# A two-axis FFT mixing followed by a squared-ReLU feed-forward: the row d = 128 is spread over the partitions by way of DRAM, two more windows form P−Q+N on VectorE, and two small copies go to GpSimd

## The chip, the cores and the metric

The kernel runs on one core of one Trainium2 chip. The metric is the device time of one execution in microseconds; the time before is 608.82 us, the median of three runs (608.44 to 608.91). A core has TensorE (PE in the profile; PEld is its weight load), VectorE (DVE), ScalarE (ACT), GpSimd (POOL) and SyncE (SP). Each engine takes its instructions in the order in which they were issued to it; semaphores join the engines. DMAs are issued from the queues of SP, ACT and POOL.

## The reference, cut to what matters

```python
# x: (8, 3008, 256) f32; w_in: (256, 2048); w_out: (2048, 256)
X = fft(fft(x, axis=1), axis=2)           # over the 3008 positions, then over the 256 channels
y = X.real.reshape(8 * 3008, 256)         # 24,064 tokens
h = maximum(y @ w_in, 0)
out = h * h @ w_out                       # (24064, 256) f32
```

The kernel computes it in f16 with f32 accumulation. A real input makes the two FFTs symmetric: frequency k and frequency S − k need the same two products, and the output column for k uses their one combination and that for S − k the other. So the kernel works on 12,040 columns (one for each pair k, S − k of every batch element) and writes two output rows from nearly every column.

## The kernel before, in words

**Order.** There is no scheduler: the order in which the Python code issues instructions is the order on each engine. The kernel cuts the 12,040 columns into 25 *windows* (`wins`, w = 0 to 24): 240, 512, 376, 376, 512 and 448 columns first, then 512 each, the last 360. Counted from one, windows 3 and 4 are the fourth and the fifth block. A window is worked through in eight *steps* s = 0 to 7; one step makes two of the sixteen 128-row groups of the hidden layer.

**What a step does.** For its two groups a plain step runs `pq(s)` (L825: four matmuls, cosine part P from `zc` and sine part Q from `zs`, 512 columns each in a full window, into the PSUM tile `ph`), then `relu(s, 0)` on ScalarE (L861) for the columns k, later `turn(s)` (L849: two more matmuls that subtract the sine part twice and add the row d = 128 with the other sign) and `relu(s, 1)` for the columns S − k; `power` (L866) squares on VectorE. Between these stand sixteen matmuls of the second layer of the window before (`ffn2_steps`, L687; twelve where that window has 376 columns), its evictions `osb` (L702) and stores (L667, on SP's queue), and a share of the work that prepares later windows (`others`, L879).

**P−Q+N steps.** In the steps listed in `diff` (L728, L760 to L763) the two `turn` matmuls are not run. There `cosines(s)` (L834) makes P alone, `twice(s)` on VectorE (L840) computes t2 = N − 2P while only P is in PSUM, `sines(s)` (L844) adds Q, and `relu(s, 1)` becomes one VectorE instruction (L859) that adds t2 and the PSUM tile and cuts at zero. `sines` has to wait for `twice`, because it overwrites what `twice` reads. The square of the first half then goes to ScalarE (`power_act`, L870), that of the second half stays on VectorE. Before, `diff` lists (4, 6) for windows 4 and 5, (0, 2, 4, 6) for most later ones, (2, 4, 6) for windows 8, 10, 13, 16 and 19, and (0, 2) for window 9: 73 such steps.

**N.** N is the contribution of the row d = 128, which sits in partition 0 of `zs` (twice, with the weight row of that channel): for hidden row f and column n it is g2n[f] · zs[0, n]. `spread_nyq(wt)` (L777) spreads partition 0 of window wt's `zs` over all 128 partitions: a matmul with the selector `sel` (L781, into a PSUM tile `pn` of the pool of two that the z matmuls use) and a copy on ScalarE (L782) into `zn`. `nyq_rows(wt, steps)` (L784) makes from it, on GpSimd, the two products of a step (L790) in a tile `n2`; there are three such buffers, so the rows of one step wait until `twice` of the third step before has read its own. `nyq` (L892) says when: for a window whose step 0 is in `diff`, `hi` is 5, the spread and the rows of its first step are issued at step 5 of the window before, the others at steps 6 and 7. For a window that starts its list at 2 it is one step later, and windows 4 and 5 do it at their own step 0.

**z.** The columns of a later window (`zc`, `zs`) are made by the z matmuls (L572) of `z_steps`, spread over the steps from `lo` up to but not including `hi` (L798; windows 3 and 4 set their own `lo` and `hi`, L813 and L817), with evictions on ScalarE (L577, L583) and VectorE (L601).

**Folds.** The even frequencies of a batch element i go through DRAM once: `away` (L456) writes `ev`, `back` (L464, L466) reads it in two orders, both on GpSimd's queue, as do the loads of x (L127, L132). `fold8`, `fold16` and `nyq8` (L473 to L497) follow on VectorE; `nyq8`, two copies of four elements per partition, is issued at step 0 of the window two after the one with `away`, and the z matmuls of that unit read what it writes.

Of the kernel before, what the change touches and what calls it, by code (L numbers as in the profile page):

```python
# [9 lines left out]
F32 = mybir.dt.float32  # L10
F16 = mybir.dt.float16
I32 = mybir.dt.int32
AF = mybir.ActivationFunctionType
# [3 lines left out]
P = 128  # L17
# [3 lines left out]
def rev_dim(ap, i):  # L21

    dims = [list(d) for d in ap.ap]
    step, cnt = dims[i]
    dims[i] = [-step, cnt]
    return bass.AP(tensor=ap.tensor, offset=ap.offset + step * (cnt - 1), ap=dims)
# [3 lines left out]
def kernel(  # L30
# [14 lines left out]
    nc = tc.nc  # L45
    B, S, D = x.shape
# [9 lines left out]
    WN = 512  # L56
# [23 lines left out]
    NW = len(wins)  # L80

    def win_of(col):
        return max(w for w in range(NW) if wins[w][0] <= col) if col < TOT else NW
# [5 lines left out]
    col_of = {}  # L89
# [11 lines left out]
    const = ctx.enter_context(tc.tile_pool(name="const", bufs=1))  # L101
# [9 lines left out]
    drp = ctx.enter_context(tc.tile_pool(name="drp", bufs=2, space=bass.MemoryType.DRAM))  # L111
    ps_h = ctx.enter_context(tc.tile_pool(name="ps_h", bufs=2, space=bass.MemoryType.PSUM))
    ps_o = ctx.enter_context(tc.tile_pool(name="ps_o", bufs=2, space=bass.MemoryType.PSUM))
    ps_z = ctx.enter_context(tc.tile_pool(name="ps_z", bufs=2, space=bass.MemoryType.PSUM))
# [72 lines left out]
    spn = fop.tile([P, 2, 2, P], F16, name="spn")  # L187
# [128 lines left out]
    for i in (1, 0):  # L316
        nc.gpsimd.tensor_scalar(out=perm[i], in0=prow_i, scalar1=float(P - 1 - i), scalar2=None, op0=ALU.is_equal)
    nc.gpsimd.dma_start(out=wout16, in_=moe_w_out.rearrange("(c p) o -> p c o", p=P))
    sel = const.tile([P, P], F16, name="sel")
    nc.gpsimd.memset(sel, 0.0)  # L320
    nc.gpsimd.memset(sel[0:1, :], 1.0)
    pick = const.tile([P, 1], F16, name="pick")
    nc.gpsimd.memset(pick, 0.0)
    nc.gpsimd.memset(pick[0:1, :], -2.0)
# [42 lines left out]
    def fold_steps(i):  # L367
# [15 lines left out]
        lo = xf[:, :, 1:129]  # L383
        hi = rev_dim(xf[:, :, 128:256], 2)
# [108 lines left out]
        def nyq8():  # L493

            xt, yt = st["xt"], st["yt"]
            nc.vector.tensor_copy(xt[:, 0, :, :, 130:131], rev_dim(rev_dim(xt[:, 1, :, :, 128:129], 1), 2))
            nc.vector.tensor_copy(spn[:, :, :, 0:1], rev_dim(yt[:, :, 0, :, 128:129], 1))  # L497

        late = [lambda: fold8(0), lambda: fold8(1), lambda: fold16(0), lambda: fold16(1), nyq8]
        return {"u_odd": u_odd, "u_part": u_part, "v_even": v_even, "v_part": v_part, "d_even": d_even, "n_cos": n_cos, "odds": odds, "d_odd": d_odd, "load": load, "n_sin": n_sin, "nyq": nyq, "even": even, "away": away, "back": back, "late": late}  # L500

    gh = const.tile([P, 3, F], F16, name="gh")
# [35 lines left out]
    def zwin(w):  # L538
        if w not in zc:
            zc[w] = zp.tile([P, WN], F16, name="zc", tag="zc")  # L540
            zs[w] = zp.tile([P, WN], F16, name="zs", tag="zs")
        return zc[w], zs[w]
# [182 lines left out]
    NST = NFC // 2  # L725
    at_of = {w: [[] for _ in range(NST)] for w in range(NW)}
    post_of = {w: [[] for _ in range(NST)] for w in range(NW)}
    diff = {w: (0, 2, 4, 6) if w > 5 else (4, 6) for w in range(4, NW)}  # L728

    def put(w, s, i, name, *k, d=at_of):  # L730
        d[w][s].append(lambda: folds[i][name](*k))
# [32 lines left out]
    n2s = {}  # L764
# [12 lines left out]
    def spread_nyq(wt):  # L777
        wn1 = wins[wt][1]
        zn = zns[wt] = znp.tile([P, WN], F16, name="zn", tag="zn")
        pn = ps_z.tile([P, 512], F32, name="pn", tag="pz")  # L780
        nc.tensor.matmul(pn[:, 0:wn1], sel, zwin(wt)[1][:, 0:wn1], start=True, stop=True)  # L781
        nc.scalar.activation(zn[:, 0:wn1], pn[:, 0:wn1], AF.Copy, bias=0.0, scale=1.0)  # L782

    def nyq_rows(wt, steps):  # L784
        wn1 = wins[wt][1]
        for s in steps:
            n2 = n2s[wt, s] = wp.tile([P, 2, WN], F32, name="n2", tag="w16")
            for a in range(2):
                fc = 2 * s + a
                nc.gpsimd.tensor_scalar(out=n2[:, a, 0:wn1], in0=zns[wt][:, 0:wn1], scalar1=g2n[:, fc : fc + 1], scalar2=1.0, op0=ALU.mult, op1=ALU.mult)  # L790

    old = None
    for w in range(NW):
# [1 line left out]
        h2 = h2p.tile([P, NFC, 2 * WN], F16, name="h2", tag="h2")  # L795
        zcw, zsw = zwin(w)

        lo, hi = int(any(win_of(col_of[i, 1]) == w + 1 for i in range(2, B))), NST - 3 if 0 in diff.get(w + 1, ()) else NST - 2  # L798
        at, post = at_of[w], post_of[w]
        if w == 1:  # L800
            fj = fold_jobs(1)
# [6 lines left out]
        elif w == 3:  # L808
# [4 lines left out]
            lo, hi = 3, NST - 1  # L813
        elif w == win_of(col_of[1, 1]) - 1:
            for st in range(5):
                at[min(st, 3)] += folds[1]["late"][st : st + 1]
            lo, hi = 4, NST - 1  # L817
# [72 lines left out]
                    j()  # L890

        def nyq(s):  # L892
            if w + 1 in diff and hi < NST - 1:
                if s == hi:
                    spread_nyq(w + 1)
                    nyq_rows(w + 1, diff[w + 1][0:1])
                elif s == hi + 1:
                    nyq_rows(w + 1, diff[w + 1][1 : 2 if s < NST - 1 else None])
                elif s == hi + 2:
                    nyq_rows(w + 1, diff[w + 1][2:])  # L900
            if s == 0 and w in diff and w not in zns:
                spread_nyq(w)
                nyq_rows(w, diff[w])

        def quad(p):
            ph = phs[p] = ps_h.tile([P, 2, 512], F32, name="ph", tag="psh")
            for c in range(4):
                f0 = (4 * p + c) * P
                o = ph[:, c // 2, (c % 2) * wn : (c % 2 + 1) * wn]
                nc.tensor.matmul(o, gh[:, 0, f0 : f0 + P], zcw[:, 0:wn], start=(c % 2 == 0), stop=False, skip_group_check=True)  # L910
                nc.tensor.matmul(o, gh[:, 1, f0 : f0 + P], zsw[:, 0:wn], start=False, stop=True, skip_group_check=True)
# [54 lines left out]
        for s in range(NST) if w > 1 else ():  # L966
            held["on"] = s + 1 in diff.get(w, ()) or (s + 1 == NST and 0 in diff.get(w + 1, ()))
            if s in diff.get(w, ()):
                cosines(s)
                twice(s)  # L970
                settle()
                others(s)
                sines(s)
                first(s)
                relu(s, 1)
                keep(s, 1, 2)
                plus.append(lambda s=s, p=power_act: p(s))
                nyq(s)
                continue
            pq(s)  # L980
            settle()
            first(s)
            if s == NST - 1:
                power(s, 0, 1)
            others(s)
            nyq(s)
            turn(s)
            relu(s, 1)
            keep(s, int(s == NST - 1), 2)
# [36 lines left out]
```

## Time and profile before

The profiled execution took 607.33 us, of which the profile spans 605.5 us; the median of the three runs shown is 608.82 us.

| | |
|---|---|
| time, median of three | 608.82 us |
| profiled execution / its span | 607.33 / 605.5 us |
| granted TensorE clock | 0.999 of full speed |
| spreading matmuls (L781) | 21 |
| copies of the spread row (L782) | 21, 616 ns each at 512 columns |
| products n2 (L790) | 146 |
| `twice` (L842) / relu on VectorE (L859) | 73 / 73 |
| copies of `nyq8` (L496, L497) | 8 and 8, 3.5 and 1.8 us in all |

The page of the profile gives the busy time of each engine, a strip of 40 time slices, the DMA queues, the chain of work that ended last, and groups of instructions by source line; the trace answers by line, tile and stretch of time. Matmuls are pipelined, so that the time one takes from its neighbour is the distance of their starts, not the length shown.

### The profile page before, as it was taken

To read this page: it belongs to the slowest core of one execution; us is meant where nothing else is said; L and a number is where in the kernel's file an instruction comes from. 1 tells how busy PE (TensorE), PEld (TensorE's weight loads), DVE (VectorE), ACT (ScalarE), POOL (GpSimd) and SP (SyncE) were. 2 spreads that over 40 slices of the span, in tenths; PEclk is the share of its full clock that TensorE was granted. 3 is DMA by queue.
4 is the path that set the end of the run, shared out by engine and by line. 5 is a ranking of instruction groups with operands and counts; after the bars stand their busy time and mean duration, and the time that the engine had idled before them with its cause. 6 is when DMAs were issued, how large, how long until landed. Compare 5 with 4: busy or idle time off the path is not lost.

```text
span 605.5 us, 11294 instructions
## 1 busy us (share of the span) xinstructions
PE 591.2 (98%) x4449; PEld 427.9 (71%) x4449; DVE 490.1 (81%) x593; ACT 462.8 (76%) x634; POOL 213.6 (35%) x249
## 2 busy tenths in 40 slices
PE   7899999999999999999999999999999999999997
PEld 3457786776777777777777767777677777777786
DVE  8787656987998878979889799888988988777760
ACT  6697777968888787877787878787777787878762
POOL 8320223245504506365045451363431522513300
PEclk9999999999999999999999999999999999999999
DMA  8945321127111361271113711146112311111112
GB/s 150 155 90 136 115 71 34 39 94 150 52 49 40 114 140 52 77 166 48 52 37 109 146 53 36 40 125 134 44 30 86 88 35 39 51 46 38 54 57 69
DMA packets 36524, 47.52 MB, mean 78 GB/s; under 512 B 4215, under 2 KB 30327, under 8 KB 36471
## 3 DMA queue, kind: packets, MB, share of 16 engines
q0 software_dynamic: 9344, 22.14, 17.9%
q1 hardware_dynamic: 26899, 24.44, 13.5%
q8 instruction: 35, 0.57, 0.4%
q10 hardware_dynamic: 228, 0.21, 0.1%
q14 instruction: 18, 0.15, 0.1%
HBM read 33.63 MB, written 27.84 MB: 102 GB/s over the span
## 4 chain that ended last, share of the span: by engine, by line
PE 87%; DVE 9%; ACT 2%; issue 1%; POOL 0%; DVEq 0%; POOLq 0%; ACTq 0%
PE po L687 49%; PE ph L852 8%; PE ph L829 7%; PE ph L830 7%; PE ph L847 5%; PE ph L838 5%; PE pz L572 4%; DVE h L868 3%; DVE t L842 2%; DVE h L859 2%; DVE xy L491 1%; PE pn L781 1%; ACT h L923 1%; ACT h L861 0%; DVE m L243 0%
## 5 line engine op out<-in xcount | busy, mean ns | idle before, releaser
L687 PE MATMUL po<-wout,h 128*128 128x256 f16 (+1 forms) x3024 | 362.3, 273 | 0.0
L861 ACT ACTIVATE h<-ph 128x1024 f16<-128x1024 f32 (+3 forms) x311 | 295.5, 993 | 79.0 <-PE ph L847 59.1
L687 PEld LDWEIGHTS <-h 128*128 128x128 f16 (+1 forms) x3024 | 296.8, 98 | 72.0
L790 POOL TENSOR_SCALAR n<-zn,g2n 128x512 f32<-128x512 f16 (+2 forms) x146 | 144.2, 1002 | 256.3 <-ACT zn L782 248.4
L868 DVE TENSOR_TENSOR h<-h 128x1024 f16<-128x1024 f16 (+6 forms) x216 | 203.2, 951 | 30.0 <-ACT h L861 27.5
L859 DVE CUSTOM_DVE_ANT_0 h<-t,ph 128x1024 f16<-128x1024 f32 x67 | 81.7, 1220 | 31.6 <-ACT h L861 31.5
L842 DVE SCALAR_TENSOR_TENSOR t<-ph,n 128x1024 f32<-128x1024 f32 (+2 forms) x73 | 87.7, 1202 | 23.4 <-PE ph L838 22.1
L829 PE MATMUL ph<-zc,gh 128*128 128x512 f16 (+3 forms) x238 | 87.4, 368 | 0.4 <-ACT h L923 0.3
L830 PE MATMUL ph<-zs,gh 128*128 128x512 f16 (+3 forms) x238 | 87.4, 368 | 0.0
L872 ACT ACTIVATE h<-h 128x1024 f16<-128x1024 f16 (+2 forms) x73 | 76.5, 1048 | 0.0
L852 PE MATMUL ph<-zs,gh 128*128 128x512 f16 (+3 forms) x238 | 68.1, 368 | 0.2 <-ACT h L861 0.2
L702 ACT ACTIVATE osb<-po 128x512 f32<-128x512 f32 (+3 forms) x95 | 55.5, 589 | 10.6 <-PE po L687 9.7
L847 PE MATMUL ph<-zs,gh 128*128 128x512 f16 (+2 forms) x146 | 42.7, 374 | 1.4 <-DVE t L842 1.2
L838 PE MATMUL ph<-zc,gh 128*128 128x512 f16 (+2 forms) x146 | 42.8, 375 | 0.4 <-DVE h L859 0.4
L830 PEld LDWEIGHTS <-gh 128*128 128x128 f16 x238 | 23.2, 98 | 25.7 <-issue 0.9
L829 PEld LDWEIGHTS <-gh 128*128 128x128 f16 x238 | 23.2, 97 | 25.0
L577 ACT ACTIVATE es<-pz 128x376 f32<-128x376 f32 (+1 forms) x32 | 14.9, 486 | 16.4 <-PE pz L572 16.3
L852 PEld LDWEIGHTS <-gh 128*128 128x128 f16 x238 | 22.3, 98 | 6.2 <-issue 0.3
L838 PEld LDWEIGHTS <-gh 128*128 128x128 f16 x146 | 14.3, 98 | 17.2 <-issue 0.6
L456 POOL DMA_DIRECT2D scr<-ev x8 | 4.9, 616 | 58.3 <-DVE ev L452 52.5
L466 POOL DMA_INDIRECT rb<-scr,idx_r x16 | 18.2, 1140 | 4.9 <-issue 4.9
L132 POOL DMA_INDIRECT xo<-in_x_dram,idx_r x15 | 16.3, 1090 | 4.5 <-issue 4.3
(145 smaller groups left out, 368.5 us busy)
## 6 DMA issues: line engine op xcount, KB each, us to landing
out_dram<-osb SPq DMA_DIRECT2D x77, 128.0 KB
xo<-in_x_dram POOLq DMA_DIRECT2D x7, 768.0 KB
scr<-ev POOLq DMA_DIRECT2D x8, 390.0 KB, 2.9
rb<-scr POOLq DMA_DIRECT2D x16, 130.0 KB
out_dram<-osb SPq DMA_DIRECT2D x12, 94.0 KB
w<-in_moe_w_in_dram POOLq DMA_DIRECT2D x2, 512.0 KB
wout<-in_moe_w_out_dram POOLq DMA_DIRECT2D x1, 1024.0 KB, 11.9
out_dram<-osb SPq DMA_DIRECT2D x8, 75.0 KB
```

What stands on the lines that cost most here:

```text
L687: nc.tensor.matmul(po[0:m, j * D : (j + 1) * D], h2[:, fc, q : q + m], wout16[:, fc, :], start=(fc == 0), stop=(fc == NFC - 1))
L790: nc.gpsimd.tensor_scalar(out=n2[:, a, 0:wn1], in0=zns[wt][:, 0:wn1], scalar1=g2n[:, fc : fc + 1], scalar2=1.0, op0=ALU.mult, op1=ALU.mult)
L829: nc.tensor.matmul(ph[:, a, 0:wn], gh[:, 0, f0 : f0 + P], zcw[:, 0:wn], start=True, stop=False)
L830: nc.tensor.matmul(ph[:, a, 0:wn], gh[:, 1, f0 : f0 + P], zsw[:, 0:wn], start=False, stop=True)
L838: nc.tensor.matmul(ph[:, a, 0:wn], gh[:, 0, f0 : f0 + P], zcw[:, 0:wn], start=True, stop=True)
L842: nc.vector.scalar_tensor_tensor(out=t2[:, :, 0:wn], in0=phs[s][:, :, 0:wn], scalar=-2.0, in1=n2s[w, s][:, :, 0:wn], op0=ALU.mult, op1=ALU ...
L847: nc.tensor.matmul(phs[s][:, a, 0:wn], gh[:, 1, f0 : f0 + P], zsw[:, 0:wn], start=False, stop=True, skip_group_check=True)
L852: nc.tensor.matmul(phs[s][:, a, 0:wn], gh[:, 2, f0 : f0 + P], zsw[:, 0:wn], start=False, stop=True, skip_group_check=True)
L859: nc.vector._custom_dve(TENSOR_ADD_SAT, out=h, in0=t2s[s][:, :, 0:wn], in1=phs[s][:, :, 0:wn], s0=BIG, s1=0.0)
L861: nc.scalar.activation(h, phs[s][:, :, 0:wn], AF.Relu, bias=0.0, scale=-1.0)
L868: nc.vector.tensor_tensor(h, h, h, op=ALU.mult)
L872: nc.scalar.activation(h, h, AF.Square, bias=0.0, scale=1.0)
```

## The change

Four things are edited. (1) `spread_nyq` no longer uses TensorE: ScalarE's queue writes the row, `zs[0:1, 0:wn1]`, to a small DRAM tile `rd` (two buffers), and GpSimd's queue reads it back with a partition step of 0, so that all 128 partitions of `zn` get it. The selector `sel` is gone. (2) The steps move: `hi` is 4 for windows before one with step 0 in `diff` (it was 5) and 5 for the others in `diff` (it was 6); the rows of the first step are issued one step after the spread, those of the second one step later again, the rest at step 7 or, where the steps run out, at step 0 of the window itself. (3) `diff` gets the steps (2, 4, 6) for window 3, which had none, and for window 4, which had (4, 6). (4) `nyq8` runs on GpSimd for batch elements i > 1.

```diff
-    sel = const.tile([P, P], F16, name="sel")
-    nc.gpsimd.memset(sel, 0.0)
-    nc.gpsimd.memset(sel[0:1, :], 1.0)
...
-            nc.vector.tensor_copy(xt[:, 0, :, :, 130:131], rev_dim(rev_dim(xt[:, 1, :, :, 128:129], 1), 2))
-            nc.vector.tensor_copy(spn[:, :, :, 0:1], rev_dim(yt[:, :, 0, :, 128:129], 1))
+            eng = nc.gpsimd if i > 1 else nc.vector
+            eng.tensor_copy(xt[:, 0, :, :, 130:131], rev_dim(rev_dim(xt[:, 1, :, :, 128:129], 1), 2))
+            eng.tensor_copy(spn[:, :, :, 0:1], rev_dim(yt[:, :, 0, :, 128:129], 1))
...
-    diff = {w: (0, 2, 4, 6) if w > 5 else (4, 6) for w in range(4, NW)}
+    diff = {w: (0, 2, 4, 6) if w > 5 else (4, 6) if w == 5 else (2, 4, 6) for w in range(3, NW)}
...
-        pn = ps_z.tile([P, 512], F32, name="pn", tag="pz")
-        nc.tensor.matmul(pn[:, 0:wn1], sel, zwin(wt)[1][:, 0:wn1], start=True, stop=True)
-        nc.scalar.activation(zn[:, 0:wn1], pn[:, 0:wn1], AF.Copy, bias=0.0, scale=1.0)
+        rd = drp.tile([1, WN], F16, name="rd", tag="rd")
+        nc.scalar.dma_start(out=rd[:, 0:wn1], in_=zwin(wt)[1][0:1, 0:wn1])
+        nc.gpsimd.dma_start(out=zn[:, 0:wn1], in_=bass.AP(tensor=rd.tensor, offset=rd.offset, ap=[[0, P], [1, wn1]]))
...
-        lo, hi = ..., NST - 3 if 0 in diff.get(w + 1, ()) else NST - 2
+        lo, hi = ..., NST - 4 if 0 in diff.get(w + 1, ()) else NST - 3 if w + 1 in diff else NST - 2
...
         def nyq(s):
-            if w + 1 in diff and hi < NST - 1:
+            if w + 1 in diff:
                 if s == hi:
                     spread_nyq(w + 1)
-                    nyq_rows(w + 1, diff[w + 1][0:1])
                 elif s == hi + 1:
-                    nyq_rows(w + 1, diff[w + 1][1 : 2 if s < NST - 1 else None])
+                    nyq_rows(w + 1, diff[w + 1][0:1])
                 elif s == hi + 2:
+                    nyq_rows(w + 1, diff[w + 1][1:2])
+                elif s == hi + 3:
                     nyq_rows(w + 1, diff[w + 1][2:])
             if s == 0 and w in diff and w not in zns:
                 spread_nyq(w)
                 nyq_rows(w, diff[w])
+            elif s == 0 and w in diff:
+                nyq_rows(w, [q for q in diff[w] if (w, q) not in n2s])
```

In the instruction lists of the two programs, TensorE loses 29 matmuls: the 21 spreads, two `turn` matmuls of 512 columns (window 4, step 2) and six of 376 (window 3). ScalarE loses 21 copies and gains 22 DMA issues, VectorE loses twelve small copies and gains four `twice` and four L859 instructions, and GpSimd gains 22 DMA issues, twelve small copies and eight products.

More of the change, by code (lines that the diff above doesn't have):

```diff
@@ L796 @@
         zcw, zsw = zwin(w)
-        lo, hi = int(any(win_of(col_of[i, 1]) == w + 1 for i in range(2, B))), NST - 3 if 0 in diff.get(w + 1, ()) else NST - 2
+        lo, hi = int(any(win_of(col_of[i, 1]) == w + 1 for i in range(2, B))), NST - 4 if 0 in diff.get(w + 1, ()) else NST - 3 if w + 1 in diff else NST - 2
         at, post = at_of[w], post_of[w]
@@ L892, in nyq @@
         def nyq(s):
-            if w + 1 in diff and hi < NST - 1:
+            if w + 1 in diff:
                 if s == hi:
                     spread_nyq(w + 1)
+                elif s == hi + 1:
                     nyq_rows(w + 1, diff[w + 1][0:1])
-                elif s == hi + 1:
-                    nyq_rows(w + 1, diff[w + 1][1 : 2 if s < NST - 1 else None])
                 elif s == hi + 2:
+                    nyq_rows(w + 1, diff[w + 1][1:2])
+                elif s == hi + 3:
                     nyq_rows(w + 1, diff[w + 1][2:])
```

## The prediction

> **What bounds the kernel.** I read the page's busy times first, then the chain that ended last, then the waits, then the stretches of time around the places that the change touches.
>
> ```profile
> PE 591.2 (98%) x4449; PEld 427.9 (71%) x4449; DVE 490.1 (81%) x593; ACT 462.8 (76%) x634; POOL 213.6 (35%) x249
> ...
> PE 87%; DVE 9%; ACT 2%; issue 1%; POOL 0%; DVEq 0%; POOLq 0%; ACTq 0%
> ```
>
> TensorE is busy 98% and carries 87% of the chain. A busy figure of pipelined matmuls may hide idle time, so I took the starts of all matmuls from the trace: 109 ns apart at 256 columns and 216 ns at 512, in unbroken series. What exceeds that between neighbours is 16.4 us in all, but only 3.4 us of it after 100 us. From there to the end the kernel is a stream of matmuls without holes, and a matmul taken out is worth its slot, if nothing that the stream waits for gets later.
>
> What a spread matmul occupies stands in a stretch of window 6 (start, length, engine, line):
>
> ```profile
> 180.13 0.59 PE L847 MATMUL ph<-zs,gh 128*128 128x512 f16 x2
> ...
> 180.56 0.38 PE L781 MATMUL pn<-zs,sel 128*128 128x512 f16 x1
> ...
> 180.78 0.38 PE L829 MATMUL ph<-zc,gh 128*128 128x512 f16 x1
> ```
>
> The 0.38 is its length in the pipeline; the next starts 0.22 after it. At 376 columns, four starts of L829 and L830 in window 3 (84.15, 84.30, 84.46, 84.62) give 0.157.
>
> **The sum on TensorE.** Out go 21 spreads: 19 × 0.216 + 0.19 (448 columns) + 0.15 (360) = 4.44. Out go two turns of 512 columns, 0.43, and six of 376, 0.95. Together **−5.83 us**. Nothing is added to TensorE.
>
> **What takes their place: the way by DRAM.** Before, N came quickly and then waited. In window 10, for step 0 of window 11:
>
> ```profile
> 250.97 0.38 PE L781 MATMUL pn<-zs,sel 128*128 128x512 f16 x1
> ...
> 251.95 0.66 ACT L782 ACTIVATE zn<-pn 128x512 f16<-128x512 f32 x1
> ...
> 252.78 1.36 POOL L790 TENSOR_SCALAR n<-zn,g2n 128x512 f32<-128x512 f16 x2 [5.58 <-ACT zn L782]
> ...
> 258.02 1.23 DVE L842 SCALAR_TENSOR_TENSOR t<-ph,n 128x1024 f32<-128x1024 f32 x1
> ```
>
> The rows are done at 254.14 and first needed at 258.02. After the change ScalarE issues the write behind the relu of step 4, which ends at 249.78: 8.24 us before that need, less the 0.22 of the spread that no longer lies between. The same distance is 8.1 to 9.3 us at all fourteen windows whose successor starts its list at step 0 (5, 6, 8, 10, 11, 13, 14, 16, 17, 19 to 23). The chain to fit in:
>
> - issue on ScalarE's queue: its last stores, L667, took 0.26 to 0.53 us; I take 0.4.
> - landing of the 1 KB row in DRAM: not in the trace. The nearest are the loads of one row (L155, L157), all landed after 1.9 us at 353.7 and after 3.5 at 426.5. I take 2.0, bounds 1.4 (the first landings of a store on ScalarE's queue) to 3.5.
> - the read of 128 × 1 KB on GpSimd's queue: the nearest is L464 (128 × 1040 B), whose landings ended 2.2 to 2.3 us after the issue in ten of sixteen, 2.7 to 5.4 in the others (5.4 at 254.1). I take 2.2.
> - two products: 1.4 uncontended; VectorE's two-input SBUF instructions hold them up (four took 5.50 at 94.82, so 2.75 for two). I take 1.4 to 2.0.
>
> Sum 6.0 to 6.6 against 8.0, and 0.3 more that the sixteen second-layer matmuls (1.75) leave behind `twice` (1.23 and some 0.2 of signal time). So the usual boundary has 1.7 to 2.3 us to spare: **cost 0**, covered by steps 5 to 7; bounds per boundary: 0 and, with the upper values (0.53 + 3.5 + 5.4 + 2.75 = 12.2), 3.9. What queues behind the waiting read on GpSimd are these products, and in fold windows the loads of `rb` and x, read by VectorE two windows later. Behind ScalarE's write stands the next relu; `zs` is finished a step before (its last VectorE pieces are let go ahead of `sines`), so it should issue at once. For windows that start their list at step 2 the distance is 13.9 us or more.
>
> I add **+0.6** for crowded DMA engines: the read that landed late at 254.1 shared its time with stores of 37 and 71 rows, and window 10 is one of the fourteen; one or two boundaries should be late by some 0.3 to 1 (bounds 0 and 4.5).
>
> **Window 4, step 2.** The new entry of window 4 is the one tight place. Its spread is issued at step 7 of window 3, behind the evictions L702.
>
> ```profile
> 91.74 0.38 ACT L702 ACTIVATE osb<-po 112x256 f32<-112x256 f32 x1
> ...
> 94.82 5.50 POOL L790 TENSOR_SCALAR n<-zn,g2n 128x512 f32<-128x512 f16 x4 [12.96 <-ACT zn L782]
> ...
> 95.66 1.60 DVE L868 TENSOR_TENSOR h<-h 128x2048 f16<-128x2048 f16 x1 [1.67 <-ACT h L861]
> ...
> 97.03 0.38 PE L829 MATMUL ph<-zc,gh 128*128 128x512 f16 x1
> ```
>
> The evictions end at 92.12, less the 0.95 saved: 91.2. The chain above lands `zn` at 95.4; the products then meet L868 and L480 and end at 97.4 to 98.1. `cosines(2)` would start at 97.03 − 0.95 − 0.22 = 95.86 and be done at 96.3; twelve second-layer matmuls (1.31) bring TensorE to `sines` at 97.6, while `twice` ends at 98.6 to 99.4. A hole of 1.0 to 1.8; I take **+1.2** (bounds 0.3, where only `twice` against 1.31 counts, and 2.5).
>
> **The four added P−Q+N steps elsewhere.** Per step of window 3 VectorE gets `twice` and L859 (0.91 each in the rows at 360 columns, the nearest to its 376) and loses half a square (0.94 to 0.55): +1.4, three times; in window 4 +1.9. From 94 to 114 us it is busy 15.6 of 20 and from 73 to 94 12.9 of 21, so it has room: cost 0, bounds 0 and 1 (`twice` behind three folds at step 1 of window 3). ScalarE loses 21 × 0.6 and a relu for each square it gains: off the path, 0.
>
> **Small copies.** VectorE loses 12 of
>
> ```profile
> L497 DVE COPY spn<-xy 128x4 f16<-128x4 f16 x8 | 3.5, 438 | 0.0
> ```
>
> and L496 (220 ns), 4 us, off the path. On GpSimd they cost about 0.35 each (its copy of 128x2, L331, took 0.34) and stand behind the products of step 6. In windows 7 and 10 the z matmuls read them one step later: in window 7 the products end at 163.8 and the first z matmul starts at 165.0, so 0.5 is left. Cost 0, bounds 0 and 2.
>
> **Sum:** 605.5 − 5.83 + 1.2 + 0.6 = 601.5 for the span. The profiled execution is 607.33, 1.8 longer than its span and 1.5 below the median; I take the change, −4.0, from the median: **604.8 us**.
>
> **A rule against it.** On GpSimd a product takes 0.69 us alone and 1.9 to 2.4 beside VectorE's two-input SBUF instructions; were the issue of the read held up in the same way, it would come 1.2 to 1.7 later. The rows of L464 do not show that: its issue takes 0.54 to 0.61 in all sixteen cases, with VectorE at its usual load. The Trainium skill, page "SBUF — State Buffer", section "SBUF: two separate sides", warns of just this: a DMA issued from GpSimd waits for its descriptors while VectorE holds the port that the two share, by its example 620 ns alone and about 3100 beside a VectorE copy. By the page's figures each read would come 2.5 us later and the fourteen boundaries would lose 0.2 to 0.8 each.
>
> **Rivals.**
>
> - *Nothing is late* (25%): window 4's products beat my chain, all else hides. 608.82 − 5.83 = 603.0. For it: 1.7 us or more of slack at the usual boundary. Against: the sum at window 4.
> - *Stores crowd the read* (12%): stores of 71, 59, 67, 79 and 41 rows go out near the critical time in windows 10, 16, 17, 21 and 22. If the read lands 3 us later there, as L464 did at 254.1, the chain is 9.2 and each of the five loses about 0.9: 608.82 − 5.83 + 1.2 + 4.5 = 608.7, no change. The Trainium skill, page "DMA: Bandwidth & Descriptors", section "Why a DMA increments its semaphore by 16 and not by 1", says that a DMA is cut over the largest number of engines, up to 16, that divides its rows. By that rule a prime count of rows goes to one engine; the late landings beside 71 and 37 rows agree.
> - *GpSimd and VectorE collide at the boundary* (7%): where the products ran 0.7 us later because of a small load (L157, 353.7), the square before `twice` took 1.17 instead of 0.69 and TensorE had a hole of 0.75, against 0.2 or none elsewhere. All products now run some 1.5 us later; 0.5 at ten boundaries gives 609.2.
> - *The round trip replaces the matmul as the wait* (12%, slower): at all fourteen boundaries `twice` waits for the products. With upper values (0.5, a write of 2.7, a read of 2.9 as the write L456 has in the median, products of 2.75) the chain is 8.85 and costs 0.55 each: 608.82 − 5.83 + 1.2 + 7.7 = 611.9. It decides from a chain of 8.6 us on, where fourteen holes of 0.3 eat what is saved.
> - *The read's issue waits for VectorE* (2%): 1.7 later at every read on top of products of 2.0 gives 8.3, no loss at most boundaries; only with products of 2.75 it is 9.05, 0.75 at each of fourteen: 608.82 − 5.83 + 1.2 + 10.5 = 614.7. This is where the rule of the page on SBUF would show.
> - That the change doesn't do what it says is excluded: the lists of instructions show 29 matmuls fewer.
>
> **Numbers.** Forecast 604.8: 42%. A measurement of this kernel can tell about 0.2% (1.2 us) from no change. Faster takes the forecast, the first rival and a little of the crowded case: 0.70; same, most of the crowded case and the collisions: 0.16; slower: 0.14. The range reaches from just below the first rival (some of the 3.4 us of holes may close) to the collisions: 602.5 to 609.5.
>
> **What would show it.** 29 matmuls fewer and PE busy near 585; starts of matmuls without new holes at the fourteen boundaries; a hole of about 1.2 us ahead of the first `sines` of window 4, ended by `twice` and behind it by the products; a wait of `twice` for the products near 2 us in all (0.5 before); the row's write landing in about 2 us and its read in 2.2. I am wrong if `twice` waits for the products at most boundaries, if the write takes 3 us, or if ScalarE stands before its DMA issue.

## The result, and the profile after

The changed kernel takes 617.5 us (616.9 to 618.24, four runs) beside 608.72 us of the kernel before on the same chip: a ratio of 1.0148, with a 95% interval of 1.0133 to 1.0163. It is 1.5% slower. The forecast of 604.8 us and its range of 602.5 to 609.5 are missed. The profiled execution took 618.08 us, with a span of 616.3.

The page of the profile after: busy times, and the chain that ended last by engine and by line.

```profile
PE 587.3 (95%) x4420; PEld 425.1 (69%) x4420; DVE 487.1 (79%) x589; ACT 452.9 (73%) x613; POOL 229.1 (37%) x289
...
PE 67%; DMA 14%; DVE 8%; POOL 4%; issue 3%; ACT 3%; POOLq 0%; ACTq 0%; DVEq 0%
PE po L685 38%; DMA zn<-rd 7%; DMA rd<-zs 6%; PE ph L850 5%; PE ph L827 5%; PE ph L828 5%; PE ph L845 5%; POOL n L788 4%; PE ph L836 4%; PE pz L570 3%; DVE t L840 3%; DMA out_dram<-osb 2%; DVE h L866 1%; ACT h L859 1%; DVE h L857 1%
```

TensorE's 29 matmuls are gone, and it is busy 95% where it was busy 98%. The chain runs less through TensorE: 67% of it, 87% before. 14% of it is DMA, and the two DMAs that lead are the two hops of the new way, the read (7%) and the write (6%). The waits say what TensorE stood for (sum in us, number, longest). First TensorE's own, then three from the list of all engines:

```profile
PE ph L845 <- DVE t L840: 12.7, 11, 1.9
...
PE ph L850 <- ACT h L859: 2.0, 3, 1.6
```

```profile
POOL zn L780 <- DMA rd<-zs: 193.6, 21, 14.8
...
POOL n L788 <- DMA zn<-rd: 77.4, 21, 5.2
...
DVE t L840 <- POOL n L788: 16.9, 14, 2.6
```

Read from below: `twice` (L840) waits for the products, the products for the read, the read for the write, and `sines` (L845) for `twice`. Before, `sines` waited 1.2 us in all for `twice`, and `twice` 0.5 for the products.

From the starts of the matmuls, the time between neighbours beyond their own slots is 33.3 us, against 16.4 before: 16.9 more, less the 5.83 saved, is 11.1; the span grew by 10.8. The holes behind this are in these places:

- ahead of the first `sines` of nine windows (7, 11, 12, 14, 15, 17, 18, 22, 23): 1.12, 2.04, 1.90, 0.28, 0.69, 1.58, 1.68, 0.37 and 1.74, 11.4 us together
- 1.81 at 157.4, in the step in which the row of window 7 is sent: the only case of a `turn` that waits because ScalarE stood for a store (2.1 us) before it issued the write of the row
- in windows 3 and 4: 1.8, 0.34 and 1.20
- two z matmuls that wait for the copies on GpSimd: 0.74 and 0.61
- 0.3 in the first 15 us; this stretch differs by more between kernels that are alike there, and nothing is concluded from it.

About 1.3 us of holes of the kernel before are filled in exchange. One boundary in full, from step 4 of window 10 to the first `sines` of window 11:

```profile
254.34 0.21 ACTq L779 DMA_DIRECT2D rd<-zs  x1
...
254.58 0.54 DVE L599 SCALAR_TENSOR_TENSOR zs<-es,pz 128x376 f16<-128x376 f32 x1
...
259.33 0.55 POOL L780 DMA_DIRECT2D zn<-rd  x1 [6.29 <-DMA rd<-zs]
...
264.99 1.36 POOL L788 TENSOR_SCALAR n<-zn,g2n 128x512 f32<-128x512 f16 x2 [5.11 <-DMA zn<-rd]
...
266.39 1.23 DVE L840 SCALAR_TENSOR_TENSOR t<-ph,n 128x1024 f32<-128x1024 f32 x1 [2.65 <-POOL n L788]
...
267.66 0.59 PE L845 MATMUL ph<-zs,gh 128*128 128x512 f16 x2 [1.87 <-DVE t L840]
```

The write of 1 KB is landed 4.5 us after its issue, the read is issued 5.0 us after the write and landed 5.5 us later, and the products are ready 12.0 us after the write was issued.

### The profile page after: what moved, and what is told of

It is laid out like the page before. It is cut to its first block, busy times and chain, and to the rows that moved or that the text cites. A ratio compares the mean times of both kernels' runs of the same rounds, so it can differ in the third digit from the quotient of the medians.

```text
span 616.3 us, 11267 instructions
## 1 busy us (share of the span) xinstructions
PE 587.3 (95%) x4420; PEld 425.1 (69%) x4420; DVE 487.1 (79%) x589; ACT 452.9 (73%) x613; POOL 229.1 (37%) x289
## 4 chain that ended last, share of the span: by engine, by line
PE 67%; DMA 14%; DVE 8%; POOL 4%; issue 3%; ACT 3%; POOLq 0%; ACTq 0%; DVEq 0%
PE po L685 38%; DMA zn<-rd 7%; DMA rd<-zs 6%; PE ph L850 5%; PE ph L827 5%; PE ph L828 5%; PE ph L845 5%; POOL n L788 4%; PE ph L836 4%; PE pz L570 3%; DVE t L840 3%; DMA out_dram<-osb 2%; DVE h L866 1%; ACT h L859 1%; DVE h L857 1%
## 5 line engine op out<-in xcount | busy, mean ns | idle before, releaser
L859 ACT ACTIVATE h<-ph 128x1024 f16<-128x1024 f32 (+3 forms) x307 | 292.0, 993 | 103.1 <-PE ph L845 82.5
L866 DVE TENSOR_TENSOR h<-h 128x1024 f16<-128x1024 f16 (+6 forms) x216 | 194.7, 912 | 22.7 <-ACT h L859 19.9
L788 POOL TENSOR_SCALAR n<-zn,g2n 128x512 f32<-128x512 f16 (+3 forms) x154 | 141.3, 930 | 81.3 <-DMA zn<-rd 77.4
L840 DVE SCALAR_TENSOR_TENSOR t<-ph,n 128x1024 f32<-128x1024 f32 (+3 forms) x77 | 91.8, 1192 | 41.2 <-PE ph L836 23.8
L827 PE MATMUL ph<-zc,gh 128*128 128x512 f16 (+3 forms) x230 | 84.7, 369 | 0.4 <-ACT h L924 0.3
L780 POOL DMA_DIRECT2D zn<-rd x22 | 12.9, 584 | 193.6 <-DMA rd<-zs 193.6
L828 PE MATMUL ph<-zs,gh 128*128 128x512 f16 (+3 forms) x230 | 84.7, 369 | 0.0
L870 ACT ACTIVATE h<-h 128x1024 f16<-128x1024 f16 (+3 forms) x77 | 79.8, 1036 | 0.0
L850 PE MATMUL ph<-zs,gh 128*128 128x512 f16 (+3 forms) x230 | 66.1, 369 | 2.0 <-ACT h L859 2.0
L700 ACT ACTIVATE osb<-po 128x512 f32<-128x512 f32 (+3 forms) x95 | 55.2, 586 | 11.1 <-PE po L685 10.9
L845 PE MATMUL ph<-zs,gh 128*128 128x512 f16 (+3 forms) x154 | 44.8, 372 | 13.0 <-DVE t L840 12.7
L836 PE MATMUL ph<-zc,gh 128*128 128x512 f16 (+3 forms) x154 | 44.8, 373 | 0.1
L828 PEld LDWEIGHTS <-gh 128*128 128x128 f16 x230 | 22.5, 98 | 25.1 <-issue 0.9
L827 PEld LDWEIGHTS <-gh 128*128 128x128 f16 x230 | 22.4, 97 | 24.4
L836 PEld LDWEIGHTS <-gh 128*128 128x128 f16 x154 | 15.0, 98 | 17.5 <-issue 0.3
L845 PEld LDWEIGHTS <-gh 128*128 128x128 f16 x154 | 14.4, 97 | 18.4 <-issue 15.7
L850 PEld LDWEIGHTS <-gh 128*128 128x128 f16 x230 | 21.7, 98 | 6.1 <-issue 2.5
```

The costliest lines, as they stand in the source:

```text
L827: nc.tensor.matmul(ph[:, a, 0:wn], gh[:, 0, f0 : f0 + P], zcw[:, 0:wn], start=True, stop=False)
L828: nc.tensor.matmul(ph[:, a, 0:wn], gh[:, 1, f0 : f0 + P], zsw[:, 0:wn], start=False, stop=True)
L836: nc.tensor.matmul(ph[:, a, 0:wn], gh[:, 0, f0 : f0 + P], zcw[:, 0:wn], start=True, stop=True)
L840: nc.vector.scalar_tensor_tensor(out=t2[:, :, 0:wn], in0=phs[s][:, :, 0:wn], scalar=-2.0, in1=n2s[w, s][:, :, 0:wn], op0=ALU.mult, op1=ALU ...
L845: nc.tensor.matmul(phs[s][:, a, 0:wn], gh[:, 1, f0 : f0 + P], zsw[:, 0:wn], start=False, stop=True, skip_group_check=True)
L850: nc.tensor.matmul(phs[s][:, a, 0:wn], gh[:, 2, f0 : f0 + P], zsw[:, 0:wn], start=False, stop=True, skip_group_check=True)
```

## Which boundaries are late

The landings differ from window to window, and the row counts of the output stores that SP issued in the 3 us ahead of the write tell which way. The table is worked out from the records of the trace (us after the issue of the write; the read from its own issue):

| to window | rows of those stores | write landed | read landed | products ready | `twice` waits |
|---|---|---|---|---|---|
| 21 | 30, 98, 128 | 1.1 | 3.4 | 7.5 | no |
| 24 | 128, 128 | 1.1 | 3.2 | 6.9 | no |
| 9 | 128, 26, 102 | 1.7 | 3.4 | 7.4 | no |
| 18 | 61, 67, 128 | 4.3 | 4.7 | 11.0 | yes |
| 12 | 123, 5, 128 | 4.4 | 5.0 | 11.3 | yes |
| 11 | 71, 57, 37, 91 | 4.5 | 5.5 | 12.0 | yes |
| 17 | 9, 94, 25, 69, 59 | 4.9 | 4.6 | 11.6 | yes |

Two stores of 128 rows do no harm; 61 and 67 rows, as many together as one of 128, do. What differs is the largest divisor up to 16: 16 for 128, 15 for 30, 14 for 98, but 1 for 61 and 67. My theory became: **the write, which is one row, stands behind stores that sit on few DMA engines.** The Trainium skill, page "DMA: Bandwidth & Descriptors", section "Why a DMA increments its semaphore by 16 and not by 1", says how many and which: a DMA takes the largest number of engines, up to 16, that divides its rows, and from ScalarE's and SP's queues the lowest-numbered ones; one row goes to the lowest. The number shows in this trace: a store of 128 rows has sixteen landings, one of 61 or 67 rows has one, besides the one that comes with the issue. Which engines they are no run here shows.

The other windows fit too, when the landings of the stores themselves are taken in place of the 3 us. The stores of 61 and 67 rows ahead of window 18 landed 7.9 and 10.4 us after their own issue. In the eight windows whose write landed after 1.1 us (4, 5, 8, 10, 13, 16, 21, 24), no store with fewer than sixteen landings was out for more than 0.2 us after the write was issued. In the thirteen other windows whose landing is on record one was, in window 19 too: its stores of 113 and 79 rows went out 4.9 and 3.7 us ahead, and its write took 3.7 us.

The rivals: any round trip by DRAM has such a latency; the step shift and the added steps cost the time; GpSimd's copies make the products late.

## The experiments

**The matmul back in the spread** (e1_matmul), at the new steps:

```diff
-        rd = drp.tile([1, WN], F16, name="rd", tag="rd")
-        nc.scalar.dma_start(out=rd[:, 0:wn1], in_=zwin(wt)[1][0:1, 0:wn1])
-        nc.gpsimd.dma_start(out=zn[:, 0:wn1], in_=bass.AP(tensor=rd.tensor, offset=rd.offset, ap=[[0, P], [1, wn1]]))
+        pn = ps_z.tile([P, 512], F32, name="pn", tag="pz")
+        nc.tensor.matmul(pn[:, 0:wn1], sel, zwin(wt)[1][:, 0:wn1], start=True, stop=True)
+        nc.scalar.activation(zn[:, 0:wn1], pn[:, 0:wn1], AF.Copy, bias=0.0, scale=1.0)
```

> The changed kernel with the selector matmul and its copy put back into the spread, at the new (earlier) steps; the added P-Q+N steps, the step shift and the copies on GpSimd stay. Theory (the two landings of the way by DRAM are late at most boundaries, everything else is nearly neutral): TensorE keeps 1.38 of the 5.83 us saved, the two waits of the z matmuls for the small copies (0.74 and 0.61) stay, the products come early, so about 0 to -1 us against before (607.5 to 609). Rival (the step shift, the z matmuls in fewer steps and the added steps in windows 3 and 4 cost the time): it stays 4 us or more above before.

Measured: 613.42 us, ratio 1.0097 (1.008 to 1.0114). My number was missed by 4 to 6 us, and the rival looked right. The waits of TensorE show why:

```profile
PE pn L782 <- DVE zs L602: 5.0, 5, 1.0
```

Five spreads (to windows 11, 14, 17, 20 and 23) stand 1.0 us each for a VectorE instruction (L602) that makes a piece of `zs`, with holes of 1.19 four times and 1.04: 5.8 us, about the whole loss (5.4). They don't wait for the row itself: by the column counts of the windows, the piece of 376 columns in the first four cases belongs to the next window. What the matmul needs is one of the two PSUM buffers that it shares with the z matmuls, and L602 still reads one. That this is the reason follows from the kernel's text; no run with a third buffer tests it. The DMA needs no such buffer: above, the write is issued at 254.34, before that piece (L599 there) starts at 254.58. Of the five, only to window 23, where 16 columns of the row come from VectorE, does its issue stand for VectorE, for 0.37 us. So the shift has a price for a matmul, and hardly one for the DMA. This run doesn't separate the landings from the rest; the next does.

**Stores cut at a multiple of 16 rows** (e3_split16), nothing else changed:

```diff
+            whole = cnt // 16 * 16
+            for at0, part_n in ((0, whole), (whole, cnt - whole)):
+                if part_n:
+                    eng.dma_start(
+                        out=bass.AP(tensor=out.tensor, offset=out.offset + (row + kstep * at0) * D, ap=[[kstep * D, part_n], [1, D]]),
+                        in_=osb[lo + at0 : lo + at0 + part_n, :])
```

> The changed kernel with every output store cut in two: the largest multiple of 16 rows, and the remainder. Nothing else changes. Theory (the 1 KB write of the row stands behind stores whose row count has no large divisor up to 16, and which therefore sit on a few engines): the write lands 1.1 to 1.6 us after its issue in nearly all windows, the 12.1 us of holes at the boundaries go, and the time falls to about 605.4 (604.5 to 607.5). Rival (a round trip by DRAM has this latency whatever the stores do; 12 further landings of 3 to 5 us are its nature): at least 614.

Measured: 604.33 us, ratio 0.9946 (0.9929 to 0.9962): 2% below the changed kernel, with 504 stores in place of 314. The write landed within 1.9 us in all windows. The landings of the read in the changed kernel (first fence; least, median, most) and with the cut (second, with the wait of `sines` left in it). These views leave out reads whose landings they can't assign, thirteen of 22 in the first; over all 22 the records give 3.1 to 5.7 us, and with the cut 3.2 to 3.7:

```profile
DMA to landing us min/median/max: 3.1/3.7/5.1
```

```profile
PE ph L848 <- DVE t L843: 2.6, 2, 1.6
...
DMA to landing us min/median/max: 3.2/3.3/3.7
```

The same boundary to window 11, with the cut:

```profile
251.31 0.20 ACTq L782 DMA_DIRECT2D rd<-zs  x1
...
253.52 0.55 POOL L783 DMA_DIRECT2D zn<-rd  x1 [3.50 <-DMA rd<-zs]
...
257.24 1.55 POOL L791 TENSOR_SCALAR n<-zn,g2n 128x512 f32<-128x512 f16 x2 [3.17 <-DMA zn<-rd]
...
260.65 1.23 DVE L843 SCALAR_TENSOR_TENSOR t<-ph,n 128x1024 f32<-128x1024 f32 x1
```

The read is issued 2.2 us behind the write where it was 5.0, and the products end 1.9 ahead of `twice`, which waits for nothing. All nine boundary holes are gone, and the one of ScalarE's stand too; left are those in windows 3 and 4, and the 0.61 of one z matmul. The round trip as such is not too long; the rival falls.

**The write from GpSimd's queue** (e4_poolwrite):

```diff
-        nc.scalar.dma_start(out=rd[:, 0:wn1], in_=zwin(wt)[1][0:1, 0:wn1])
+        nc.gpsimd.dma_start(out=rd[:, 0:wn1], in_=zwin(wt)[1][0:1, 0:wn1])
```

> The changed kernel with the write of the row issued from GpSimd's queue in place of ScalarE's. Theory (the write is queued behind stores on the same few DMA engines): from another queue it uses other engines in most windows, the write lands in some 2 us, ScalarE never stands before its issue, and most of the 12.1 us of boundary holes go: 605 to 611. Rival (the latency is that of two hops on any queue): 614 or more, since GpSimd adds an issue of about 0.5 us.

Measured: 616.49 us, ratio 1.0147 (1.0126 to 1.0167), as the changed kernel. My expectation failed. First the wait of `sines`, then how long the write took to land (least, median, most):

```profile
PE ph L845 <- DVE t L840: 12.2, 10, 2.5
```

```profile
DMA to landing us min/median/max: 1.6/3.5/7.4
```

From this queue the trace has sixteen landings for the one row, not one, and the last of them counts: to window 12 the first came 3.9 us after the issue and the last 7.4. The same page and section of the Trainium skill says that a DMA from GpSimd posts its end on all 16 engines, whatever its shape; the sixteen landings agree. So this write, too, waits for the last of the engines. My idea of "other engines" was wrong; queueing behind the stores still fits, but this run alone doesn't show it.

**One hop, from partition 0 of SBUF to all partitions** (e6_onehop):

```diff
+        row = zwin(wt)[1][0:1, 0:wn1]
+        nc.gpsimd.dma_start(out=zn[:, 0:wn1], in_=row.unsqueeze(1).to_broadcast([1, P, wn1]))
```

> The changed kernel with the way by DRAM replaced by one DMA on GpSimd's queue that copies the row from partition 0 of SBUF to all 128 partitions. Theory (the sum of two landings is what is late; the second alone took 3.1 to 5.7 us and products 1.4 to 2.4, against about 9 us available): no boundary waits, 604 to 606. Rival 1 (one landing beside stores is late already): the holes of windows 11, 12, 17, 18, 23 stay in part, 608 to 612. Rival 2 (128 reads of one partition are slow): landing above 7 us, 614 or more.

Measured: 608.42 us, ratio 1.0005 (0.9994 to 1.0016): rival 1's number. The wait of `sines`, and the DMA's landing (last figure, the median of the windows with 512 columns):

```profile
PE ph L844 <- DVE t L839: 6.3, 7, 1.5
```

```profile
zn<-zs POOLq DMA_DIRECT2D x19, 128.0 KB, 7.1
```

One landing in place of two removes half of the waits, not all, and it is a slow landing: 5.2 to 11.4 us over all windows, the most to windows 11 and 17. With cut stores (e13_onehop_split16, below) it is 5.2 to 7.3, where the two landings of e3_split16 together are 4.2 to 5.2. A good part of rival 2 is true as well.

**The kernel before with the stores cut** (e5_before_split16), the control; the edit is that of e3_split16.

> The kernel before, with only its output stores cut in two (a multiple of 16 rows, and the remainder). Control: how much of the 13 us that the cut brought to the changed kernel does it bring without the way by DRAM? Theory (the cut matters only because the row's write lands behind the stores): the kernel before has no wait on a small transfer at its boundaries, so nothing to win: 607.5 to 608.7, within 0.2% of before. Rival (slow stores hold up the kernel in general, by late buffers or late loads): 604 or less.

Measured: 607.31 us, ratio 0.9981 (0.997 to 0.9992), 0.2 below my range. So 1 of the 13 us is a gain of its own. Where it lies is not shown: the profiled execution was the slowest of the ten (608.51), and its last landing comes 3.34 us after its last matmul, 3.17 before. With the way by DRAM the cut does shorten this end, from 3.25 in the changed kernel to 2.2 in e3_split16. The other 12 us exist only with the way by DRAM.

**The way by DRAM and its step shift alone, stores cut** (e7_dram_alone_split16): e3_split16, with

```diff
-    diff = {w: (0, 2, 4, 6) if w > 5 else (4, 6) if w == 5 else (2, 4, 6) for w in range(3, NW)}
+    diff = {w: (0, 2, 4, 6) if w > 5 else (4, 6) for w in range(4, NW)}
...
-            eng = nc.gpsimd if i > 1 else nc.vector
+            eng = nc.vector
```

> The way by DRAM and the step shift alone (no further P-Q+N steps in windows 3 and 4, small copies on VectorE), with the stores cut as before this run at 604.3. Theory: the holes of 1.77, 1.20 and 0.34 us in windows 3 and 4 and of 0.61 at a z matmul go, eight turns (1.38) come back: 604.3 - 3.9 + 1.4 = 601.8 (600.8 to 603). Rival (the added steps and the copies pay, as the prediction's sum had them): 605 or more.

Measured: 601.2 us, ratio 0.9886 (0.9861 to 0.9912), as expected. The last matmul ends at 596.18, and at 602.36 in the control: 6.18 us earlier, of which the 21 spreads are 4.44 and holes 1.75 (15.9 us of them against 17.7). Beside e3_split16's 604.33 it is 3.1 us less: the added steps and the copies on GpSimd, the two edits taken out, cost together; they don't pay.

**One of these edits back at a time**, stores whole. The small copies on VectorE (e9_copies_back, the second edit above):

> The changed kernel with the small copies back on VectorE, all else as changed. Theory: the waits of the z matmuls for GpSimd's copies (0.74 and 0.61 us) go and the 12 us at the boundaries stay: about 616.2 (615 to 617). Rival (GpSimd's extra work is what makes the products late): 613 or less.

Measured: 616.96 us, ratio 1.0133 (1.0106 to 1.016). The z matmuls wait for no copy any more, and `sines` still waits 12.8 us for `twice`. In time it can't be told from the changed kernel; that the copies make the products late is ruled out.

The added P−Q+N steps taken out (e10_steps_back, the first edit above):

> The changed kernel without the added P-Q+N steps of windows 3 and 4, all else as changed. Theory: the holes of 1.8, 1.2 and 0.34 go, eight turns (1.38) come back, the boundaries stay: about 615.5 (614.5 to 616.8). Rival (as predicted, the added steps pay little less than their 1.38): 617.5 or more.

Measured: 615.69 us, ratio 1.0111 (1.0084 to 1.0139). The intervals touch, so the time alone leaves it open; the holes in windows 3 and 4 are gone in its trace. What they were shows in window 3, step 2, of the changed kernel:

```profile
77.53 1.60 DVE L477 TENSOR_TENSOR xy<-rb 128x1040 f16<-128x1040 f16 x2
...
79.16 0.43 DVE L488 TENSOR_TENSOR xy<-xy 128x520 f16<-128x520 f16 x1
...
79.51 0.93 DVE L840 SCALAR_TENSOR_TENSOR t<-ph,n 128x752 f32<-128x752 f32 x1
...
80.50 0.48 PE L845 MATMUL ph<-zs,gh 128*128 128x376 f16 x2 [1.64 <-DVE t L840]
```

`twice` stands behind three folds in VectorE's order: no landing plays a part.

**The cut at a prime** (e11_split_prime): about as many pieces as in e3_split16 (535 stores, there 504), but nearly all rows of an uneven store on a count without divisors.

```diff
-            whole = cnt // 16 * 16
+            whole = cnt if cnt % 16 == 0 or cnt < 3 else max(n1 for n1 in range(2, cnt) if all(n1 % f for f in range(2, n1)))
```

> The changed kernel with every store whose row count is no multiple of 16 cut in two at the largest prime below its count (71 = 67 + 4, 94 = 89 + 5). As many DMAs, with the same bytes in total, as with the cut at a multiple of 16, which ran at 604.3. Theory (rows of a store without a divisor sit on one engine, and the row's landing waits for that engine): the landings get as late as in the changed kernel or later, more windows wait, 618 to 640. Rival (what helped was smaller or more DMAs, whatever engines they use): about 604.3, at most 608.

Measured: 761.85 us, ratio 1.2533 (1.2512 to 1.2553); the sign is the theory's, the size far beyond my range. First the chain by line, then a wait:

```profile
SPq L668 23%; DMA out_dram<-osb 21%; PE po L688 15%; DMA zn<-rd 5%; DMA rd<-zs 4%; PE ph L853 3%; PE ph L830 3%; PE ph L831 3%; ACT h L862 3%; PE ph L848 2%; POOL n L791 2%; DVE t L843 2%; ACT h L873 1%; PE ph L839 1%; ACT osb L703 1%
```

```profile
ACT h L862 <- DMA out_dram<-osb: 90.8, 12, 15.8
```

The write of the row lands 3.2 to 4.4 us after its issue in all 21 windows whose landing is on record; with the cut at 16 it was 1.9 at most. But `sines` waits only 13.6 us for `twice`, not much more than in the changed kernel. What the 144 us more are spent on is, for the most part, the stores themselves: ScalarE stands for them 90.8 us, 2.1 in the changed kernel, and their landings and their issues on SP (SPq) make up 44% of the chain. The same bytes in nearly the same number of pieces run at 604 or at 762 us, by the row counts. That smaller or more DMAs helped is ruled out. (The granted clock of this run is 0.916, in the changed kernel 0.996; how much of the size is due to that is open.)

**One hop with cut stores** (e13_onehop_split16) and **with whole stores** (e14_onehop_alone), both without the added steps and with the copies on VectorE.

> One DMA from SBUF to SBUF for the spread, stores cut at a multiple of 16, no further P-Q+N steps, small copies on VectorE; with the two hops by DRAM the same ran at 601.2. Theory: with the cut no boundary waits any more, so a shorter chain hides the same: 600.2 to 602.2. Rival (two hops still cost somewhere, through ScalarE's issues or the shift of other loads): below 600.

> The same with whole stores. Theory: against the one-hop kernel that ran at 608.4, the added steps and the copies give back 2.6 to 3.3 us, the late landings of the one hop (6.3 us of waits of the sines in that trace, 2.7 of them in windows 3 and 4) keep about 3.6: 605 to 606.5, faster than before by 2 to 3. Rival (once the other edits are gone the copies and steps change the boundaries): outside 604 to 607.5.

Measured: 603.49 us, ratio 0.9917 (0.99 to 0.9935), and 606.54, ratio 0.9972 (0.9959 to 0.9985). The first is above its range and not below the two hops' 601.2, so two hops cost nothing hidden; it is rather above that, with boundary holes of 0.51, 0.48 and 0.58 that e7's trace lacks, though the intervals touch. The second is at the edge of its range, with holes of 1.3 and 1.5 left at windows 11 and 17.

**Steps 4 and 6 of window 3 as P−Q+N** (e15_window3_46), on e7:

```diff
-    diff = {w: (0, 2, 4, 6) if w > 5 else (4, 6) for w in range(4, NW)}
+    diff = {w: (0, 2, 4, 6) if w > 5 else (4, 6) for w in range(3, NW)}
```

> The kernel that ran at 601.2 (way by DRAM, cut stores) with P-Q+N steps 4 and 6 in window 3, away from the folds that hold VectorE up at step 2. Theory: four turns of 376 columns go, 0.63 us, and VectorE has room there: 600.6 (600.0 to 601.2). Rival (late products or VectorE at step 4): 601.5 to 602.5.

Measured: 601.11 us, ratio 0.9888 (0.9871 to 0.9904). It can't be told from e7: a new hole of 0.35 at 93.7 takes half of the 0.63. This and e7 are the fastest versions, 1.1% below the kernel before.

## Why the prediction was wrong, step by step

- **−5.83 us on TensorE**: right. 29 matmuls fewer; the 21 spreads alone, 4.44, are found again in e7.
- **The way by DRAM, cost 0 at the usual boundary**: this is the step that failed, by its two landings. The write was put at 2.0 us from the loads of one row; it took 1.1 with the engines free and up to 4.9 behind uneven stores. The read was put at 2.2 from L464; it took 3.1 to 5.7. Nine of fourteen boundaries waited, 11.4 us, and a tenth hole of 1.81 came from ScalarE before its issue. The text had the upper values, and 12.2 for their sum; window 11 measured 12.0. For the write, the error was to take the middle of rows measured beside other traffic for the usual case. For the read, L464 was the wrong neighbour: its rows in the trace of the kernel before hold only 2 to 11 of the sixteen landings, and even in e3_split16, where the same read of `rb` takes 2.4 us in the median, the read of `zn` takes 3.3. Why a read that repeats one row for all partitions is slower is not tested. With cut stores the chain is 7.5 us against 9.3 available: the slack of 1.8 is what I forecast (1.7 to 2.3), but by luck, through two errors, a chain too short by 1 and a distance too short by 1.
- **"`zs` is finished a step before, so it should issue at once"**: right at the fourteen boundaries but for window 23, where the issue stood 0.37 us for VectorE's piece of the row. What the text didn't have is that the issue can stand for a store, as it did ahead of window 7, for 2.1 us.
- **+0.6 for crowded engines**: the right cause at the wrong size. The rival of stores that crowd the read (12%) named the rule and five windows; it was wrong in two ways. The write suffers as much as the read, being one row, and row counts with a small divisor do harm as well as primes, so that more boundaries were late. Its 608.7 fell short by 9.
- **Window 4, step 2, +1.2**: right, in size (1.20) and cause: `twice` waits there for the products.
- **The other added steps, 0 (bounds 0 and 1)**: wrong. Window 3, step 2, lost 1.8, by the three folds that the bound itself had named for step 1.
- **Small copies, 0 (bounds 0 and 2)**: within the bounds; 0.74 and 0.61 in windows 7 and 10, where only 0.5 was left.
- **The rival in which the read's issue waits for VectorE (2%)**: no sign of it. The issue of the read took 536 to 622 ns in all 22 cases (median 594), as L464's did.
- **The rival that came true** is that the round trip replaces the matmul as the wait (12%). It gave 611.9, with 0.55 at each of fourteen boundaries; nine averaged 1.27 (11.4), and window 3, ScalarE's stand ahead of window 7 and the copies added what it had left out.

## What to carry over

In these runs a small DMA came late when stores of uneven row counts were still out, so look at the row counts of what is in flight, not at the bytes: cut stores at a multiple of 16 rows before a short transfer goes on the critical path. Price a landing that the trace doesn't show by the rows at the place where it will be, with the traffic that is there; a middle over quiet and crowded places is right for neither. When a step moves earlier, check in the trace, for every window, that its input is finished by then and that the buffers it writes are free.

## What the runs showed of the hardware that I had not expected

- A 1 KB write to DRAM from ScalarE's queue lands in 1.1 us with free engines and in up to 4.9 behind stores of uneven row counts.
- The same write from GpSimd's queue has sixteen landings and is done with the last, 1.6 to 7.4 us.
- A DMA that spreads one SBUF partition over 128 took 5.2 to 11.4 us, and 5.2 to 7.3 with cut stores; by way of DRAM, with cut stores, write and read took 1.1 to 1.9 and 3.2 to 3.7.
- The changed kernel with stores cut at primes is 25% slower than the kernel before; with stores cut at multiples of 16 its last landing comes 2.2 us after the last matmul in place of 3.25.
